# Remainder queries of a head pair: two 64-column products side by side, or one of full width

## The chip, the core and the metric

The kernel runs as one program on one core of a Trainium2 chip. The metric is the device time of one execution in microseconds, and the kernel before was timed three times: 865.73, 865.88 and 868.37 us, median 865.88. A smaller number is better. One further execution was recorded by the hardware profiler; all rows below come from it.

## The reference

Three stages follow each other. q is pooled over pairs of positions, so each of 4 x 8 heads has 576 queries, 1152 keys and 64 features:

```python
q_pool = q.reshape(B, H, S // 2, 2, D).mean(axis=3)
scores = scale * np.matmul(q_pool, k.transpose(0, 1, 3, 2))
attn = np.exp(scores - scores.max(-1, keepdims=True))
attn = attn / (attn.sum(-1, keepdims=True) + 1e-09)
x = np.matmul(attn, v)            # then (B*S/2, H*D) = (2304, 512)
g = x @ w_gate                    # gated layer, 512 -> 1536 -> 512
x = (g / (1 + np.exp(-g)) * (x @ w_val)) @ w_out
# soft mixture: phi (512 x 32), 8 experts of 512 -> 1024 -> 512, combined per token
```

## The kernel before, in words

**Tiling.** Heads go in 16 pairs, called steps: `(b, p)` with b of 4 batches and p of 4 pairs. The 576 queries of a head are 512, handled as four tiles of 128, and a remainder of 64 (`REM`). The keys are nine chunks of 128. A *unit* is one score tile of up to 512 columns: its products (lines 461 and 462: high and low halves of the numbers, fp16), its exponential on ScalarE (467, `P32`), and the difference between the fp32 exponential and its upper half, `PL`, on GpSimd or VectorE (474). A step has nine units for each head's 512 queries and three for the remainder: in these, a unit holds three key chunks, and of each chunk 64 columns for head 0 and 64 columns for head 1, side by side.

**Weights times values.** The exponentials are then the stationary operand (keys on partitions, queries as columns) and the values move. For the 512 queries that is `pv`, three products of 65 or 64 columns for each query tile and chunk (505, 506, 507): upper half times high values, upper half times low values, `PL` times high values. Column 65 of the values is a one, so the row sums come along. For the remainder it is `pv_rem` (497): each product has 64 stationary columns, those of head 0 write partitions 0 to 63 of slot 4 of the accumulator `acc`, those of head 1 partitions 64 to 127, and the two heads' products are issued in turn. A few units skip the split and take fp32 operands in one product.

**Finish and turn.** After head 1's last product `finish` (520 on) divides by the row sums on VectorE (535 to 537), rounds to fp16 on ScalarE (`xh`, through `cast`, line 211) and takes the rest on VectorE (`xl`, 547). Five ticks later `turn` moves tokens from partitions to columns: the 512 queries by a DMA transpose (576), the remainder by four TensorE transposes of 64 x 64 (586: two halves of the number, two heads), one per quadrant of the array, and one ScalarE copy of the result into the tile `xT` of the gated layer.

**Order.** The program order of each engine is made by a scheduler at build time from the priorities of the units, from `later(n, ...)` (n ticks on) and `not_before`. TensorE takes in turn the scores, the weights times values, the row maxima of the step after next (380), and from step 4 on the gated layer of finished tokens (738 to 743, 811, 816). Engines execute in that order. `acc` has one PSUM bank (`PVB` is 1), so the next head's first `pv` waits until `finish` has read it. The transposes and the logits of the gated layer share one bank (`tr`).

The stationary tile of an instruction stands in the rows as 128*128 or 128*64: contraction rows times stationary columns.

Of the kernel before, what the change touches and what calls it, by code (L numbers as in the profile page):

```python
# [10 lines left out]
F16 = mybir.dt.float16  # L11
F32 = mybir.dt.float32
# [5 lines left out]
ALU = mybir.AluOpType  # L18
# [59 lines left out]
def tile_pool_attention_glu_softmoe(  # L78
# [52 lines left out]
    def not_before(ins, lead):  # L131

        if len(marks) > lead >= 0:
            after(ins, marks[-1 - lead])
# [133 lines left out]
    def split_pair(b, p, first=None):  # L268
        if not first and (b, p) not in highs:
            split_high(b, p)  # L270
        kr, qr, vr = raw[b, p]
        i = (b * NP + p) % NKQ
        KL = KLs[i]
        VV = at.tile([P, 2, NCH, 2, D + 1], F16, tag="VV", bufs=2, name=f"VV{b}_{p}")
        KK = at.tile([P, 2, S], F16, tag="KK", bufs=2, name=f"KK{b}_{p}")
        QQ = at.tile([P, 2, SQ], F16, tag="QQ", bufs=2, name=f"QQ{b}_{p}")
        QH = at.tile([D + 1, 2, SQ], F16, tag="QH", bufs=2, name=f"QH{b}_{p}")
        QHs[b, p] = QH
        for hd in range(2):
            st[b, p, hd] = (KK[:, hd, :], KL[:, hd, :], QQ[:, hd, :], QH[:, hd, :], VV[:, hd], vr[:, hd])  # L280
        if first:
            first_split(*first, KK[:, 0, :], KL[:, 0, :], QQ[:, 0, :], QH[:, 0, :])
            maxima(9)

        if first:
            split_high(b, p, first)
        del raw[b, p]
        r, qp, kh, qh, q_cast = highs.pop((b, p))
        ql = at.tile([P, SQ], F16, tag="ql", bufs=1, name=f"ql{b}_{p}")
        q_low = sub("l", b, p).tensor_tensor(out=ql[r], in0=qp, in1=qh[r], op=ALU.subtract).ins.name  # L290
        kl = at.tile([P, S], F16, tag="kl", bufs=1, name=f"kl{b}_{p}")
        k_low = nc.gpsimd.tensor_tensor(out=kl[r], in0=kr[r], in1=kh[r], op=ALU.subtract)
# [183 lines left out]

    def pv_rem(acc, PH, PL, b, p, parts):

        for i in range(0, len(parts), 2):
            c = parts[i][1]  # L480
            todo = []
            for z in range(2):
                dst = acc[z * D:(z + 1) * D, 4, :]
                VV, vr = st[b, p, z][4:]
                q = slice((i + z) * REM, (i + z + 1) * REM)
                if PL is None:
                    todo.append([(dst, PH[:, q], vr[:, c, :])])
                else:
                    todo.append([
                        (dst[:, :D + 1], PH[:, q], VV[:, c, 0, :]),  # L490
                        (dst[:, :D], PH[:, q], VV[:, c, 1, :D]),
                        (dst[:, :D + 1], PL[:, q], VV[:, c, 0, :]),
                    ])
            n = len(todo[0])
            for k in range(n):
                for z in range(2):
                    nc.tensor.matmul(  # L497
                        *todo[z][k], start=False, stop=(c == NCH - 1 and k == n - 1), skip_group_check=True
                    )

    def pv(dst, PH, PL, VV, vr, q, c, first):
        if PL is None:
# [18 lines left out]
    def attn(b, p):  # L521
# [1 line left out]
        acc = {}  # L523

        def finish(hd):
            ns = 4 + hd
            t = acc[hd]
            if hd == 0:
                acc["x"] = at.tile([P, 5, 2, 2, D], F16, tag="xhl", bufs=XB, name=f"xhl{b}_{p}")
            xhl = acc["x"]  # L530
            rs = at.tile([P, 5, 1], F32, tag="rs", bufs=2, name=f"rs{b}_{p}_{hd}")
            x32 = at.tile([P, 5, D], F32, tag="x32", bufs=1, name=f"x32{b}_{p}_{hd}")

            with tc.high_priority(offset=HP_F):
                nc.vector.tensor_scalar(rs[:, :ns, :], t[:, :ns, D:D + 1], EPS * PSC, 1.0 / XSC, ALU.add, ALU.mult)
                nc.vector.reciprocal(out=rs[:, :ns, :], in_=rs[:, :ns, :])
                nc.vector.tensor_tensor(  # L537
                    out=x32[:, :ns, :], in0=t[:, :ns, :D], in1=rs[:, :ns, :].to_broadcast([P, ns, D]), op=ALU.mult
                )
            xh, xl = (xhl[:, :ns, i, hd, :] for i in range(2))  # L540

            def high():
                not_before(cast("x", b, p, xh, x32[:, :ns, :]), 0)

            def low():
                not_before(
                    sub("x", b, p).tensor_tensor(out=xl, in0=x32[:, :ns, :], in1=xh, op=ALU.subtract), 0
                )

            later(2, high)  # L550
            later(3, low)
            if hd:
                later(5, lambda: turn(xhl))

        def pv_unit(parts, PH, PL):
            hd, c, q0, w = parts[-1]
            if q0 < QT:
                VV, vr = st[b, p, hd][4:]
                if c == 0:
                    acc[hd] = ps("pv", [P, 5, D + 1], bufs=PVB, name=f"pv{b}_{p}_{hd}")  # L560
                for q in range(QT // P):
                    pv(acc[hd][:, q, :], PH, PL, VV, vr, slice(q * P, (q + 1) * P), c, c == 0 and q == 0)
            else:
                pv_rem(acc[1], PH, PL, b, p, parts)
            if hd == 0 and c == NCH - 1 and q0 < QT:
                finish(0)
            if hd == 1 and c == NCH - 1 and q0 == QT:
                finish(1)

        def turn(xhl):  # L570

            for g in range(2):
# [9 lines left out]
            tx = ps("tr", [P, 2, REM], F16, bufs=TRB, name=f"tx{b}_{p}")  # L582
            for hl in range(2):
                for z in range(2):
                    r = slice(z * D, (z + 1) * D)
                    not_before(nc.tensor.transpose(tx[r, hl, :], xhl[r, 4, hl, 1, :], id16[r, r]), 0)
            cast("t", b, p, xt_tile(NBLK - 1)[:, p, b // 2, :, b % 2 * REM:b % 2 * REM + REM], tx)
            if p == NP - 1:
                ready.extend(range(len(ready), 2 * (b + 1) if b < B - 1 else NBLK))

# [677 lines left out]
def _layout(q, k, v, moe_w_gate, moe_w_val, moe_w_out, moe2_phi, moe2_w1, moe2_w2):  # L1268
    import numpy as np

    b, h, s, d = q.shape
    vp = v.reshape(b, h // 2, 2, s // 128, 128, d).transpose(0, 1, 4, 2, 3, 5)
# [33 lines left out]
```

## Time and profile before

| | |
|---|---|
| median of three runs | 865.88 us |
| span of the profiled execution (first to last instruction) | 863.9 us |
| mean granted TensorE clock over the span | 0.990 |
| TensorE busy | 816.8 us (95%) in 9952 products |
| VectorE, ScalarE, GpSimd busy | 541.2, 392.5, 414.0 us |

The profiled execution is one execution; its span is 863.9 us, and 2.0 us lie around it if its whole time is the median. In a timeline, the start of the next row less the start of a row is what a product costs its engine, since products overlap; the duration of a product in a row is its way through the array and is longer. A busy share of TensorE therefore also holds time in which the array waits for its own pipeline.

### The profile page before, as it was taken

What the parts mean: (1) busy time and instruction counts of PE and PEld (TensorE: products, weight loads), DVE (VectorE), ACT (ScalarE), POOL (GpSimd) and SP (SyncE); (2) the same over time, 40 slices, a digit from 0 to 9 for tenths busy, and PEclk for the clock granted to TensorE, in tenths of its full rate; (3) what the DMA queues carried; (4) which work ended last, traced back from release to release, by engine and by line L of the source; (5) the groups of instructions that cost most, each with busy time, mean ns of one, the idle gap of its engine ahead of it and who ended that gap; (6) DMA issues with size and microseconds to landing.
All of it is one profiled execution on the core that took longest, in us unless ns stands there. A gap on an engine that the chain in (4) does not pass through costs nothing.

```text
span 863.9 us, 23702 instructions
## 1 busy us (share of the span) xinstructions
PE 816.8 (95%) x9952; PEld 580.0 (67%) x9952; DVE 541.2 (63%) x1060; ACT 392.5 (45%) x739; POOL 414.0 (48%) x380
## 2 busy tenths in 40 slices
PE   5888898999999999999999999999999999998997
PEld 1455566777666767677776777676777777776345
DVE  6878779678888675666657575666723444445223
ACT  3455678677778444343434344344434211212112
POOL 7878667465768545564564556565445100000100
PEclk9999999999999999999999999999999999999998
DMA  6562678959759433424544445324012598457999
GB/s 194 149 153 84 200 214 239 284 127 280 192 173 293 115 61 82 111 76 100 130 115 120 111 107 125 65 26 97 16 28 38 149 292 267 85 165 193 297 290 292
DMA packets 151868, 132.48 MB, mean 153 GB/s; under 512 B 83152, under 2 KB 120720, under 8 KB 151760
## 3 DMA queue, kind: packets, MB, share of 16 engines
q1 hardware_dynamic: 149600, 130.92, 57.8%
q8 instruction: 78, 1.28, 0.6%
q10 hardware_dynamic: 2160, 0.04, 0.1%
q14 instruction: 30, 0.25, 0.1%
HBM read 84.10 MB, written 7.86 MB: 106 GB/s over the span
## 4 chain that ended last, share of the span: by engine, by line
PE 75%; DVE 12%; DMA 7%; ACT 3%; issue 2%; SPq 0%; ACTq 0%; DVEq 0%
PE st L462 7%; PE st L461 7%; PE mx L380 6%; PE g L738 5%; PE g L743 5%; PE g L742 5%; PE v L738 5%; PE v L743 5%; PE v L742 5%; DVE mp L386 3%; PE pv L497 3%; PE pv L505 3%; PE pv L506 3%; PE pv L507 3%; PE hp L1179 2%
## 5 line engine op out<-in xcount | busy, mean ns | idle before, releaser
L474 POOL TENSOR_TENSOR PL<-P 128x512 f16<-128x512 f32 (+1 forms) x311 | 326.0, 1061 | 230.0 <-ACT P L467 227.7
L467 ACT ACTIVATE P<-st 128x512 f32<-128x512 f32 (+1 forms) x336 | 191.4, 582 | 207.0 <-PE st L462 174.1
L386 DVE TENSOR_REDUCE mp<-mx 128x1 f32<-128x512 f32 x270 | 179.9, 684 | 55.9 <-PE mx L380 53.0
L461 PE MATMUL st<-QQ,KK 128*128 128x512 f16 (+1 forms) x576 | 143.7, 291 | 5.1 <-ACT P L467 4.3
L462 PE MATMUL st<-QH,KL 65*128 65x512 f16 (+1 forms) x576 | 144.4, 293 | 2.7 <-DMA QH<-mt 2.7
L505 PE MATMUL pv<-VV,P 128*128 128x65 f16 x1088 | 136.8, 193 | 4.9 <-DVE x L537 4.8
L506 PE MATMUL pv<-VV,P 128*128 128x64 f16 x1088 | 136.7, 195 | 0.0
L507 PE MATMUL pv<-VV,PL 128*128 128x65 f16 x1088 | 134.6, 192 | 0.0
L738 PE MATMUL g<-xT,wgv 128*128 128x256 f16 x432 | 118.6, 275 | 3.3 <-DVE hs L750 3.0
L505 PEld LDWEIGHTS <-P 128*128 128x128 bf16 x1088 | 103.9, 98 | 25.3 <-DVE x L537 6.5
L743 PE MATMUL g<-xT,wgv 128*128 128x256 f16 x432 | 118.5, 274 | 0.5 <-DVE wgv L703 0.5
L742 PE MATMUL g<-xT,wgv 128*128 128x256 f16 x432 | 118.6, 274 | 0.0
L738 PE MATMUL v<-xT,wgv 128*128 128x256 f16 x432 | 117.9, 273 | 0.0
L743 PE MATMUL v<-xT,wgv 128*128 128x256 f16 x432 | 117.8, 273 | 0.0
L742 PE MATMUL v<-xT,wgv 128*128 128x256 f16 x432 | 117.7, 273 | 0.0
L507 PEld LDWEIGHTS <-PL 128*128 128x128 f16 x1088 | 103.7, 99 | 13.5 <-issue 4.4
L506 PEld LDWEIGHTS <-P 128*128 128x128 bf16 x1088 | 103.2, 98 | 10.4 <-issue 2.2
L380 PE MATMUL mx<-kh,QD 128*128 128x512 f16 x270 | 103.8, 402 | 6.6 <-DVE mp L386 3.1
L738 PEld LDWEIGHTS <-wgv 128*128 128x128 f16 x864 | 85.1, 98 | 18.6 <-issue 2.1
L742 PEld LDWEIGHTS <-wgv 128*128 128x128 f16 x864 | 84.8, 98 | 18.4 <-issue 4.1
L743 PEld LDWEIGHTS <-wgv 128*128 128x128 f16 x864 | 84.8, 98 | 16.1 <-issue 0.8
L462 PEld LDWEIGHTS <-KL 65*128 65x128 f16 x576 | 51.7, 99 | 33.0 <-issue 14.9
(184 smaller groups left out, 1192.4 us busy)
## 6 DMA issues: line engine op xcount, KB each, us to landing
w<-in_w SPq DMA_DIRECT2D x16, 1024.0 KB, 7.6
w<-in_w SPq DMA_DIRECT2D x64, 256.0 KB, 5.5
vr<-in_vP SPq DMA_DIRECT2D x16, 585.0 KB, 5.1
KK<-kh SPq DMA_DIRECT2D x62, 144.0 KB, 2.6
qr<-in_qT SPq DMA_DIRECT2D x15, 576.0 KB, 3.9
kr<-in_kT SPq DMA_DIRECT2D x15, 576.0 KB, 4.2
r<-in_w_out SPq DMA_DIRECT2D x12, 512.0 KB, 4.3
r<-in_w_gate SPq DMA_DIRECT2D x24, 256.0 KB, 5.1
```

Source lines behind the costliest of these rows:

```text
L380: nc.tensor.matmul(t, q, kh[:, k0:k0 + kw], start=True, stop=True)
L386: nc.vector.reduce_max(out=mp[:, g, c:c + 1], in_=t, axis=AX.X)
L461: nc.tensor.matmul(t[:, o:o + w], KK[:, k], QQ[:, q0:q0 + w], start=True, stop=False)
L462: nc.tensor.matmul(t[:, o:o + w], KL[:, k], QH[:, q0:q0 + w], start=False, stop=True)
L467: marks.append(nc.scalar.activation(P32[:, :o], t[:, :o], AF.Exp, scale=1.0 / 16.0).ins.name)
L474: eng.tensor_tensor(out=PL[:, :o], in0=P32[:, :o], in1=PH[:, :o], op=ALU.subtract)
L505: nc.tensor.matmul(dst[:, :D + 1], PH[:, q], VV[:, c, 0, :], start=first, stop=False, skip_group_check=True)
L506: nc.tensor.matmul(dst[:, :D], PH[:, q], VV[:, c, 1, :D], start=False, stop=False, skip_group_check=True)
L507: nc.tensor.matmul(dst[:, :D + 1], PL[:, q], VV[:, c, 0, :], start=False, stop=(c == NCH - 1), skip_group_check=True)
L738: mm = nc.tensor.matmul(o, w[:, 0, d, f], xh, start=(d == 0), stop=False)
L742: nc.tensor.matmul(o, w[:, 0, d, f], xl, start=False, stop=False)
L743: nc.tensor.matmul(o, w[:, 1, d, f], xh, start=False, stop=(d == ND - 1))
```

## The change

The values of the two heads of a pair are stored in reversed order (`_layout`), and `st` keeps the tile of both heads. `pv_rem` now takes all 128 columns of a chunk as stationary operand, and both heads' values (2 x 65 or 2 x 64 columns) move, so that `acc` has six slots: slot 4 holds the values of head 1, slot 5 those of head 0, and of each only one half of the partitions is used afterwards. `finish(1)` divides six slots, rounds the sixth on ScalarE and takes its rest on GpSimd, each in an instruction of its own. `turn` makes two transposes of 128 x 128 in place of four of 64 x 64, and two copies of 64 partitions in place of one of 128.

```diff
-            todo = []
-            for z in range(2):
-                dst = acc[z * D:(z + 1) * D, 4, :]
-                VV, vr = st[b, p, z][4:]
-                q = slice((i + z) * REM, (i + z + 1) * REM)
...
-                        (dst[:, :D + 1], PH[:, q], VV[:, c, 0, :]),
-                        (dst[:, :D], PH[:, q], VV[:, c, 1, :D]),
-                        (dst[:, :D + 1], PL[:, q], VV[:, c, 0, :]),
+        VV, vr = st[b, p, 1][4:]
+        dst = acc[:, 4:, :]
...
+            q = slice(i * REM, (i + 2) * REM)
+                    (dst, PH[:, q], VV[:, :, c, 0, :]),
+                    (dst[:, :, :D], PH[:, q], VV[:, :, c, 1, :D]),
+                    (dst, PL[:, q], VV[:, :, c, 0, :]),
...
-            ns = 4 + hd
+            ns = 4 + 2 * hd
...
-            xh, xl = (xhl[:, :ns, i, hd, :] for i in range(2))
+            nm = 4 + hd
+            xh, xl = (xhl[:, :nm, i, hd, :] for i in range(2))
+            rh, rl = (xhl[:, 4, i, 0, :] for i in range(2))
 
             def high():
+                if hd:
+                    not_before(cast("x", b, p, rh, x32[:, nm, :]), 0)
             def low():
+                if hd:
+                    not_before(nc.gpsimd.tensor_tensor(out=rl, in0=x32[:, nm, :], in1=rh, op=ALU.subtract), 0)
...
             for hl in range(2):
-                for z in range(2):
-                    r = slice(z * D, (z + 1) * D)
-                    not_before(nc.tensor.transpose(tx[r, hl, :], xhl[r, 4, hl, 1, :], id16[r, r]), 0)
-            cast("t", b, p, xt_tile(NBLK - 1)[:, p, b // 2, :, b % 2 * REM:b % 2 * REM + REM], tx)
+                not_before(nc.tensor.transpose(
+                    tx[:, hl].rearrange("p z n -> p (z n)"), xhl[:, 4, hl].rearrange("p z d -> p (z d)"), id16
+                ), 0)
+            for z in range(2):
+                r = slice(z * D, (z + 1) * D)
+                cast("t", b, p, xt_tile(NBLK - 1)[r, p, b // 2, :, b % 2 * REM:b % 2 * REM + REM], tx[r, :, z, :])
```

Line numbers shift by four after `pv_rem`: its products stand at 493 (before 497), those of `pv` at 501 to 503 (before 505 to 507).

The order on TensorE at the first remainder unit of step (3, 1), before: `P_1_18` and `PL_1_18` are the unit's exponentials, `st_2_1` a score tile of the next step, and a size of 64x65 is 64 partitions by 65 columns.

```order
L461 LDWEIGHTS KK_2_9943
L461 MATMUL st_2_1_10855<-QQ_2_9944,KK_2_9943 128x512
L497 LDWEIGHTS P_1_18_10671
L497 MATMUL pv_1_1_10496<-VV_1_9076,P_1_18_10671 64x65
L462 LDWEIGHTS KL_101
L462 MATMUL st_2_1_10855<-QH_2_9945,KL_101 128x512
L497 LDWEIGHTS P_1_18_10671
L497 MATMUL pv_1_1_10496<-VV_1_9076,P_1_18_10671 64x65
```

One product of the unit stands alone between two score products, and the others follow in pairs. The same unit of the changed kernel on TensorE (`lp` are logits of the gated layer):

```order
L820 LDWEIGHTS W2S
L820 MATMUL lp_4_10508<-hs_4_10396,W2S 32x256
L493 LDWEIGHTS P_1_18_10351
L493 MATMUL pv_1_1_10176<-VV_1_8808,P_1_18_10351 128x130
L493 LDWEIGHTS P_1_18_10351
L493 MATMUL pv_1_1_10176<-VV_1_8808,P_1_18_10351 128x2x64
L493 LDWEIGHTS PL_1_18_10353
L493 MATMUL pv_1_1_10176<-VV_1_8808,PL_1_18_10353 128x130
```

Each pair became one product of 128 partitions by 130 or 128 columns, and the unit stands together behind the logits.

The order on TensorE at the turn of step (3, 0), before (`tx` is the result, `xhl` the two halves of the quotient):

```order
L506 MATMUL pv_1_0_10137<-VV_1_9076,P_1_1_10013 128x64
L507 LDWEIGHTS PL_1_1_10015
L507 MATMUL pv_1_0_10137<-VV_1_9076,PL_1_1_10015 128x65
L586 LDWEIGHTS xhl_0_9542
L586 MATMUL tx_0_10182<-id_66,xhl_0_9542 64x64
```

The other three transposes of the turn follow there at once. The second transpose of the same turn in the changed kernel, forty rows behind the first:

```order
L503 MATMUL pv_1_0_9818<-VV_1_8808,PL_1_3_9792 128x65
L586 LDWEIGHTS xhl_0_9248
L586 MATMUL tx_0_9863<-id_66,xhl_0_9248 128x128
L461 LDWEIGHTS KK_1_8809
L461 MATMUL st_1_7_9955<-QQ_1_8810,KK_1_8809 128x512
```

The two transposes of a turn were separated, and the second, which reads what GpSimd makes, stands behind the products of chunk 3.

The order on GpSimd at the same turn in the changed kernel (`VV_2` is the low half of the values of the next step):

```order
L474 TENSOR_TENSOR PL_1_4_9808<-P_1_4_9806 128x512
L308 TENSOR_TENSOR VV_2_9648<-vr_2_9049,VV_2_9648 128x18x64
L474 TENSOR_TENSOR PL_1_5_9876<-P_1_5_9874 128x512
L550 TENSOR_TENSOR xhl_0_9248<-x_0_1_9780,xhl_0_9248 128x64
L474 TENSOR_TENSOR PL_1_6_9919<-P_1_6_9917 128x512
```

Line 550 is the new subtraction; the rows around it are those of before.

## Rows read from the trace of the kernel before

**Rows 1.** busy time by stretch; columns: stretch, length, each engine's busy us

```profile
0.00:150.00 150.00, 123.06 (x1498) 78.69 (x1499) 118.05 (x195) 89.64 (x163) 113.24 (x105) 0.97 0.62 176
150.00:300.00 150.00, 144.76 (x1924) 104.27 (x1923) 121.42 (x223) 107.40 (x206) 95.48 (x82) 1.00 0.77 208
300.00:691.00 391.00, 388.50 (x4895) 286.33 (x4893) 234.75 (x463) 161.87 (x304) 202.77 (x178) 1.00 0.38 88
```

**Rows 2.** longest TensorE wait, 300 to 700 us

```profile
PE mx L380 <- DVE mp L395: 0.8, 2, 0.4
```

**Rows 3.** busy time by stretch of line 497 alone

```profile
0.00:150.00 150.00, 4.66 (x160) 3.51 (x160) 0.97 0.62 176
150.00:300.00 150.00, 8.19 (x230) 5.76 (x228) 1.00 0.77 208
300.00:691.00 391.00, 22.31 (x458) 13.86 (x458) 1.00 0.38 88
```

**Rows 4.** groups by line and shape: xcount | busy us, mean ns | idle before

```profile
L497 PE MATMUL pv<-VV,P 128*64 128x65 f16 x270 | 24.5, 202 | 0.0
L497 PE MATMUL pv<-vr,P 128*64 128x65 f32 x36 | 2.1, 232 | 0.0
L586 PE MATMUL tx<-id,xhl 64*64 64x64 f16 x64 | 5.5, 208 | 0.3 <-DVE xhl L547 0.3
L505 PEld LDWEIGHTS <-P 128*128 128x128 bf16 x1088 | 103.9, 98 | 25.3 <-DVE x L537 6.5 <-issue 3.8 <-DVE xhl L547 0.2
```

**Rows 5.** TensorE timeline, one batch of remainder products; columns: start us, us, what

```profile
588.76 0.22 PE L497 MATMUL pv<-VV,P 128*64 128x65 f16 x1
588.91 0.39 PE L462 MATMUL st<-QH,KL 65*128 65x512 f16 x1
589.23 0.25 PE L497 MATMUL pv<-VV,P 128*64 128x65 f16 x3
...
589.39 0.22 PE L497 MATMUL pv<-VV,PL 128*64 128x65 f16 x2
...
589.49 0.22 PE L497 MATMUL pv<-VV,PL 128*64 128x65 f16 x2
589.64 0.65 PE L380 MATMUL mx<-kh,QD 128*128 128x512 f16 x2
```

**Rows 6.** TensorE timeline, full-width products of different kinds in succession

```profile
309.80 0.38 PE L461 MATMUL st<-QQ,KK 128*128 128x512 f16 x1
310.01 0.38 PE L462 MATMUL st<-QH,KL 65*128 65x512 f16 x1
310.23 0.19 PE L505 MATMUL pv<-VV,P 128*128 128x65 f16 x1
310.26 0.19 PE L506 MATMUL pv<-VV,P 128*128 128x64 f16 x1
```

**Rows 7.** TensorE timeline, full-width products of 128 columns (line 837)

```profile
795.31 0.62 PE L837 MATMUL warm<-id 128*128 128x128 f16 x8
...
797.43 1.07 PE L837 MATMUL warm<-id 128*128 128x128 f16 x16
```

**Rows 8.** TensorE timeline, the four small transposes of one turn

```profile
360.69 0.19 PE L507 MATMUL pv<-VV,PL 128*128 128x65 f16 x1
360.82 0.25 PE L586 MATMUL tx<-id,xhl 64*64 64x64 f16 x4
361.00 0.20 PE L505 MATMUL pv<-VV,P 128*128 128x65 f16 x1
```

**Rows 9.** groups by line and shape, other engines, around finish and turn

```profile
L537 DVE TENSOR_TENSOR x<-pv,rs 128x320 f32<-128x320 f32 x16 | 7.8, 486 | 0.3
L211 ACT COPY xT<-tx 128x128 f16<-128x128 f16 x16 | 4.3, 267 | 5.9 <-PE tx L586 5.9
```

**Rows 10.** GpSimd timeline before a turn

```profile
553.59 1.28 POOL L474 TENSOR_TENSOR PL<-P 128x512 f16<-128x512 f32 x1
```

**Rows 11.** TensorE timeline after the same turn

```profile
555.82 0.19 PE L507 MATMUL pv<-VV,PL 128*128 128x65 f16 x1
```

More of the change, by code (lines that the diff above doesn't have):

```diff
@@ L279, in split_pair @@
         for hd in range(2):
-            st[b, p, hd] = (KK[:, hd, :], KL[:, hd, :], QQ[:, hd, :], QH[:, hd, :], VV[:, hd], vr[:, hd])
+            st[b, p, hd] = (KK[:, hd, :], KL[:, hd, :], QQ[:, hd, :], QH[:, hd, :], VV, vr)
         if first:
@@ L477, in pv_rem @@
     def pv_rem(acc, PH, PL, b, p, parts):
+        VV, vr = st[b, p, 1][4:]
+        dst = acc[:, 4:, :]
         for i in range(0, len(parts), 2):
             c = parts[i][1]
-            todo = []
-            for z in range(2):
-                dst = acc[z * D:(z + 1) * D, 4, :]
-                VV, vr = st[b, p, z][4:]
-                q = slice((i + z) * REM, (i + z + 1) * REM)
[L486 to L489, printed above, removed]
-                        (dst[:, :D + 1], PH[:, q], VV[:, c, 0, :]),
-                        (dst[:, :D], PH[:, q], VV[:, c, 1, :D]),
-                        (dst[:, :D + 1], PL[:, q], VV[:, c, 0, :]),
-                    ])
-            n = len(todo[0])
-            for k in range(n):
-                for z in range(2):
-                    nc.tensor.matmul(
-                        *todo[z][k], start=False, stop=(c == NCH - 1 and k == n - 1), skip_group_check=True
-                    )
+            q = slice(i * REM, (i + 2) * REM)
+            if PL is None:
+                todo = [(dst, PH[:, q], vr[:, :, c, :])]
+            else:
+                todo = [
+                    (dst, PH[:, q], VV[:, :, c, 0, :]),
+                    (dst[:, :, :D], PH[:, q], VV[:, :, c, 1, :D]),
+                    (dst, PL[:, q], VV[:, :, c, 0, :]),
+                ]
+            for k, t in enumerate(todo):
+                nc.tensor.matmul(
+                    *t, start=False, stop=(c == NCH - 1 and k == len(todo) - 1), skip_group_check=True
+                )
     def pv(dst, PH, PL, VV, vr, q, c, first):
@@ L530, in finish @@
             xhl = acc["x"]
-            rs = at.tile([P, 5, 1], F32, tag="rs", bufs=2, name=f"rs{b}_{p}_{hd}")
-            x32 = at.tile([P, 5, D], F32, tag="x32", bufs=1, name=f"x32{b}_{p}_{hd}")
+            rs = at.tile([P, 6, 1], F32, tag="rs", bufs=2, name=f"rs{b}_{p}_{hd}")
+            x32 = at.tile([P, 6, D], F32, tag="x32", bufs=1, name=f"x32{b}_{p}_{hd}")
             with tc.high_priority(offset=HP_F):
@@ L539, in finish @@
                 )
-            xh, xl = (xhl[:, :ns, i, hd, :] for i in range(2))
+            nm = 4 + hd
+            xh, xl = (xhl[:, :nm, i, hd, :] for i in range(2))
+            rh, rl = (xhl[:, 4, i, 0, :] for i in range(2))
             def high():
-                not_before(cast("x", b, p, xh, x32[:, :ns, :]), 0)
+                not_before(cast("x", b, p, xh, x32[:, :nm, :]), 0)
+                if hd:
+                    not_before(cast("x", b, p, rh, x32[:, nm, :]), 0)
             def low():
                 not_before(
-                    sub("x", b, p).tensor_tensor(out=xl, in0=x32[:, :ns, :], in1=xh, op=ALU.subtract), 0
+                    sub("x", b, p).tensor_tensor(out=xl, in0=x32[:, :nm, :], in1=xh, op=ALU.subtract), 0
                 )
+                if hd:
+                    not_before(nc.gpsimd.tensor_tensor(out=rl, in0=x32[:, nm, :], in1=rh, op=ALU.subtract), 0)
             later(2, high)
@@ L557, in pv_unit @@
             if q0 < QT:
-                VV, vr = st[b, p, hd][4:]
+                VV, vr = (x[:, 1 - hd] for x in st[b, p, hd][4:])
                 if c == 0:
-                    acc[hd] = ps("pv", [P, 5, D + 1], bufs=PVB, name=f"pv{b}_{p}_{hd}")
+                    acc[hd] = ps("pv", [P, 6, D + 1], bufs=PVB, name=f"pv{b}_{p}_{hd}")
                 for q in range(QT // P):
@@ L581, in turn @@
                 cast("t", b, p, x, tx)
-            tx = ps("tr", [P, 2, REM], F16, bufs=TRB, name=f"tx{b}_{p}")
+            tx = ps("tr", [P, 2, 2, REM], F16, bufs=TRB, name=f"tx{b}_{p}")
             for hl in range(2):
-                for z in range(2):
-                    r = slice(z * D, (z + 1) * D)
-                    not_before(nc.tensor.transpose(tx[r, hl, :], xhl[r, 4, hl, 1, :], id16[r, r]), 0)
-            cast("t", b, p, xt_tile(NBLK - 1)[:, p, b // 2, :, b % 2 * REM:b % 2 * REM + REM], tx)
+                not_before(nc.tensor.transpose(
[4 more added lines that the diff above has]
+                cast("t", b, p, xt_tile(NBLK - 1)[r, p, b // 2, :, b % 2 * REM:b % 2 * REM + REM], tx[r, :, z, :])
             if p == NP - 1:
@@ L1271, in _layout @@
     b, h, s, d = q.shape
-    vp = v.reshape(b, h // 2, 2, s // 128, 128, d).transpose(0, 1, 4, 2, 3, 5)
+    vp = v.reshape(b, h // 2, 2, s // 128, 128, d)[:, :, ::-1].transpose(0, 1, 4, 2, 3, 5)
     return {
```

## The prediction

> **What bounds the kernel now.** I read the busy time by stretch first. TensorE is busy 123 of the first 150 us, 145 of the next 150 and 388.5 of the 391 us from 300 to 691 [rows 1]. The reader is to see that the other engines have room in the long third stretch: VectorE 235, GpSimd 203, ScalarE 162 of 391. The waits come second: between 300 and 700 us the longest thing that TensorE waited for adds up to 0.8 us [rows 2]. So from 300 us on TensorE's own queue sets the pace, from 150 us nearly so, and in the first 150 us others hold it up too. Busy doesn't mean streaming, though, so I went on to the timeline and took the time from one start to the next as a product's price.
>
> Full-width products cost what their columns cost: two of 512 columns stand 0.22 us apart, one of 65 columns 0.03 us before the next, and going from line 462 to line 505 adds nothing [rows 6]. At the remainder it is different. The line 462 product at 588.91 has 512 columns as well, but the next, 64 stationary columns wide, starts 0.32 us later: 0.10 us too late. The last pair starts at 589.49 (its second product some ns on) and the next full-width product at 589.64, 0.15 us for a pair that costs 0.03 us inside the batch: 0.12 too much. The product alone at 588.76 pays both for one product's work [rows 5]. The small transposes do the same: 0.13 us from a 65-column product into them, 0.10 over its price [rows 8]. So each change between the full and a divided array costs about 0.10 us, and TensorE counts it as busy.
>
> **What the change removes.** Counted in the program's order, the width of the array changes 541 times before and 297 times after. Of the 244 that go, 214 lie at the ends of 107 batches of line 497 and 46 at those of 23 batches of transposes; 16 are not won, since the neighbour there is a narrow product too (the logits, as in the order shown: the change into the logits stays). At 0.10 us that is -24.4 us; with 0.12 on leaving it would be -26.8, and I keep the lower price.
>
> The Trainium skill, in TensorEngine Tiling (Array Packing), Tiling Modes, says that changing the mode drains the engine, which names the cause; it gives no price.
>
> **What it adds on TensorE.** Two products side by side become one with twice the moving columns, so the packing is given up. Before, the pairs run together: from 589.39 to 589.49 lies one chunk, three pairs, 33 ns a pair [rows 5]. There are three fp16 groups of 270 products [rows 4], 810 in all, 405 pairs: 13.4 us. After, 405 products of 130 or 128 columns. Sixteen products of 128 columns take 1.07 us and eight 0.62, which is 56 ns each [rows 7]; the row of 512 columns scaled to 130 gives 56, and two 65-column products in a row 60 [rows 6]. I take 57: 23.1 us, bounds 22.5 and 25. That is +9.7. The fp32 remainder has 36 records, 18 pairs [rows 4], whose spacing no row shows alone: between nothing and twice the fp16 difference, 0 to +2 us; +0.5, near the fp16 rows. Four small transposes take 0.18 us with the way out [rows 8], so 0.08 without; 16 turns are 1.3 us, against 32 full transposes at 56 ns, 1.8: +0.5.
>
> Together on TensorE: -24.4 + 9.7 + 0.5 + 0.5 = -13.7 us.
>
> A rule speaks against this. TensorE: Matmul & The Clock Gate, Back-to-back issue gap, in the Trainium skill puts a sustained stream of weight loads and 128-column products at about 81 ns each, not 56. The line 837 rows alternate loads and products and stand at 56 ns [rows 7], so the trace doesn't agree here. By the rule the 405 products would take 32.8 us and the sum on TensorE be -4.0.
>
> **The other engines.** ScalarE gets a second copy per turn, 0.267 us for the full one and no less assumed for half the partitions, and a rounding of 64 columns, between nothing and the same 0.267 of 128 columns [rows 9]; 16 times both is up to 8.5 us, on an engine that is busy 162 of 391 us. GpSimd gets 16 subtractions of 64 columns, each between nothing and the 1.28 us of 512 columns [rows 10]; near 0.2 by share. On VectorE the product with the row sums grows from 320 to 384 columns: at most 0.1 us more on 0.486 [rows 9]. Three places could reach TensorE. The accumulator's one bank is held 0.1 us longer per step; scores and the gated layer stand in TensorE's queue meanwhile and hide it; uncovered it costs 1.6 us. The `tr` bank is held for the second copy, 0.27 us; the logits behind it wait only if they are next, 4.3 us if always. The second transpose now waits for GpSimd. Behind it stand all later products on TensorE, so this one is dangerous. In the trace of before, the GpSimd row that stands ahead of the new subtraction of step (3, 0) ends at 553.59 + 1.28 = 554.87, so its result is there at about 555.1; TensorE comes to the transpose's new place, behind the products of chunk 3, at 555.82 [rows 10, 11]: 0.7 us of slack. I laid the new order over the old times for all 16 turns; this is the tightest, others have about 2 to 5 us. The copies, the bank and this wait together I take at +0.8, between 0 and 6. SP's queue gets nothing new, and no DMA is added.
>
> **What reaches the end.** Line 497's busy time lies with 4.7, 8.2 and 22.3 us in the three stretches [rows 3]: 13, 23 and 63%. In the first, where TensorE idles 27 of 150 us [rows 1], I let half be lost: 0.9 of 1.8. In the second 15%, 0.5 of 3.2. In the third all counts, since nothing else is near its limit; what is late next there is the row maxima on VectorE, which already end that 0.8 us. From 691 us on no changed instruction runs, and the stretch starts when TensorE has finished the gated layer, so it moves up as a whole. -13.7 + 1.4 + 0.8 = -11.5. The profiled execution spans 863.9 us, and 2.0 lie around it up to the median 865.9; so 852.4 in the profile and 854.4 as time.
>
> **Rivals.**
> *The other engines take part of it.* Row maxima, exponentials and GpSimd set the pace up to 300 us, so that only 63% of 13.7 is won: 8.6 us, and less with all small waits: 857.3, up to 863. For it: VectorE is busy 121 of the 150 us in the second stretch. Against: so is TensorE 145.
> *The wide product costs more.* Each needs a load of 128 x 128 weights, which takes 98 ns [rows 4] and goes on beside the product ahead. If it is only half hidden beyond 57 ns, a product costs 78, and 405 lose 8.5 us of the 11.5: 862.9; wholly bare, at 98, 871. Against it: 65-column products with the same loads stand 30 ns apart [rows 6]. For it: no row has 130 columns from two places. The Trainium skill's 81 ns (the section above) would give 864.1.
> *GpSimd makes it slower.* Place: the second transpose of each turn. If one more difference of 1.28 us slips ahead of the new subtraction and the slack is gone, each turn stalls TensorE by 1.28 us: 16 turns, +20.5 and -11.5, 874.9. It decides from a stall of 0.72 us per turn. Against it stands the slack above.
> *The change doesn't remove the stall.* If the 0.10 us belonged not to the width but to what `pv_rem` reads or writes, 10.7 us of wider products would be added for nothing: 876.6. Against it: lines 505 to 507 read the same kind of tile and accumulate in the same bank without it [rows 6], and the transposes, which read something else, show it [rows 8].
>
> **How the numbers follow.** Forecast 0.75, its own range 850.5 to 858. The other engines 0.14, the wide product 0.05, GpSimd 0.04, no removal 0.02. A measurement of this kernel can tell about 0.3%, 2.6 us, from no change, so faster ends at 863.3: the forecast and the first rival, 0.89. The wide product straddles that edge and I count it as no change, 0.05; slower are the last two, 0.06. With both prices at their better end (0.12 on leaving, 22.5 us, nothing lost) it is some 849, with the small waits at their worse end 861; the range is 849.5 to 861.
>
> **What would show it.** Right: TensorE products of the remainder, 414 in the program, 128*128 with 130 columns, some 57 ns apart, with 0.22 us and not 0.32 between a 512-column product and the first of a batch; TensorE's span from 300 us to the last remainder shorter by about 9 us. The step on GpSimd is wrong if a wait of the transposes for the new subtraction stands in TensorE's list of waits with more than 1 us. The forecast is wrong if the remainder products stand 80 ns apart, or if the idle time of TensorE before 300 us grows by more than 3 us.

## The result, and the profile after

The change makes the kernel faster. Over 18 runs of each the median went from 865.81 to 861.53 us (852.71 to 866.75), 4.3 us less; the ratio is **0.9908, 95% interval 0.9885 to 0.9931**, which is 8.0 us, 6.0 to 10.0. All ratios here and below leave out the runs marked as slow: 865.62 and 866.75 us of after, 874.54 of before (beside experiments 9 and 10) and 2658.91 us in experiment 7. The forecast was 854.4, 11.5 us less than before, so the direction held and 3.5 us are missing by the ratio, 7.1 by the median, which lies half a us above the range's upper end, 861.0. The spread is itself a result. The three of the 18 runs whose mean granted clock of TensorE was 0.989 took 852.7, 852.9 and 853.9 us, 12 to 13 below before; those at 0.974 to 0.979 took 861 to 867. The profiled one is of the second kind: clock 0.975, span 863.3 us, time 865.11, against 0.990 and a span of 863.9 in the profiled execution of before. Its trace has to be read with that in mind: at almost the same length it shows the gain and what takes it back side by side.

First the same stretches as in [rows 1], in after (columns as there).

```profile
0.00:150.00 150.00, 123.62 (x1359) 79.75 (x1360) 110.70 (x186) 85.79 (x158) 109.01 (x104) 0.93 0.61 171
150.00:300.00 150.00, 142.23 (x1802) 105.04 (x1799) 123.60 (x227) 114.03 (x224) 101.97 (x89) 0.99 0.72 206
300.00:691.00 391.00, 387.10 (x4729) 295.42 (x4727) 240.37 (x474) 165.95 (x324) 208.06 (x189) 0.99 0.41 95
```

The granted clock (third figure from the end) is 0.93 in the first stretch where it was 0.97. As the work moves against fixed stretches, they don't show what a piece of it costs. So I cut both traces at two points of the program: VectorE's product of the accumulator with the row sums in the 8th and in the 16th (last) step. TensorE alone, before; columns: stretch, length, busy us, clock, DMA share, GB/s.

```profile
0.00:306.40 306.40, 274.22 (x3482) 0.98 0.69 190
306.40:676.90 370.50, 369.38 (x4698) 1.00 0.37 83
676.90:863.90 187.00, 173.23 (x1776) 0.98 0.85 233
```

The same between the same points, after.

```profile
0.00:310.40 310.40, 276.25 (x3250) 0.96 0.67 188
310.40:669.90 359.50, 358.22 (x4479) 1.00 0.38 85
669.90:863.30 193.40, 177.74 (x1773) 0.95 0.81 225
```

In the middle, at full clock, after is 11.0 us shorter, and all of that is busy time (369.4 to 358.2). Up to the 8th step it is 4.0 longer: 2.0 of busy time at a lower clock, 2.0 of idle time. From the last step on it is 6.4 longer, 4.5 of it busy time at clock 0.95 instead of 0.98, though only the last of the 16 turns was changed there. -11.0 + 4.0 + 6.4 = -0.6, the difference of the spans. (Up to the first point 324 products of the gated layer are done where before had 333; at 0.11 us each that is 1 us of work moved into the middle.)

The products themselves came out as forecast. TensorE's timeline in after, a batch between products of the gated layer (columns as in [rows 5]):

```profile
667.84 0.27 PE L746 MATMUL g<-xT,wgv 128*128 128x256 f16 x1
667.94 0.22 PE L493 MATMUL pv<-VV,PL 128*128 128x130 f16 x1
668.00 0.28 PE L493 MATMUL pv<-VV,P 128*128 128x130 f16 x2
668.12 0.22 PE L493 MATMUL pv<-VV,PL 128*128 128x130 f16 x1
...
668.35 0.28 PE L493 MATMUL pv<-VV,P 128*128 128x130 f16 x2
668.47 0.27 PE L747 MATMUL g<-xT,wgv 128*128 128x256 f16 x1
```

The 256-column product ahead takes 0.10 us, no more than between two of its kind, and leaving the batch costs nothing over the last product's own price. Nine products from 667.94 to 668.47 are 59 ns each here, and over the trace the median from one to the next is 58. In [rows 5] the way in cost 0.10 and the way out 0.12. It is so throughout the middle: from a 512-column score product to the first product of a batch the median is 0.22 us in after (25 places) and 0.32 in before (47). The small transposes are gone as a stall too; a turn's first transpose in after, which answers to [rows 8]:

```profile
595.38 0.19 PE L503 MATMUL pv<-VV,PL 128*128 128x65 f16 x1
595.41 0.22 PE L586 MATMUL tx<-id,xhl 128*128 128x128 f16 x1
595.47 0.38 PE L380 MATMUL mx<-kh,QD 128*128 128x512 f16 x1
```

0.03 us before it and 0.06 for it, nothing else. Counted in the order of the trace, the array's width changes 583 times before and 340 times after: 243 fewer (the forecast had 244, from the program's order).

The groups that answer to [rows 4, 9], after (columns as there): the wide products, the turn's copies and transposes, GpSimd's new subtraction and the product on VectorE.

```profile
L493 PE MATMUL pv<-VV,P 128*128 128x130 f16 x135 | 26.5, 219 | 0.0
L533 DVE TENSOR_TENSOR x<-pv,rs 128x384 f32<-128x384 f32 x16 | 8.8, 552 | 0.3
L211 ACT COPY xT<-tx 64x128 f16<-64x128 f16 x32 | 8.2, 257 | 5.6 <-PE tx L586 5.4
L550 POOL TENSOR_TENSOR xhl<-x,xhl 128x64 f16<-128x64 f32 x16 | 7.4, 460 | 4.9 <-ACT xhl L211 4.9
L586 PE MATMUL tx<-id,xhl 128*128 128x128 f16 x32 | 6.7, 223 | 0.8 <-ACT xhl L211 0.4 <-POOL xhl L550 0.3
```

And what TensorE waited for between 300 and 672 us, after, which answers to [rows 2] (columns: total us, times, longest):

```profile
PE g L742 <- DVE hs L754: 0.8, 2, 0.4
PE tx L586 <- ACT xhl L211: 0.4, 1, 0.4
PE tx L586 <- POOL xhl L550: 0.3, 1, 0.3
```

GpSimd's subtraction takes 0.46 us, more than twice my share of the 512 columns, and still TensorE waits for it once in this window, 0.3 us. The two waits of the transposes here belong to the last turn, at 671 and 672 us; between the 8th and the 16th step no transpose waits. The dangerous place of the forecast costs next to nothing.

### The profile page after: what moved, and what is told of

Its sections match the earlier page's. It is cut to its first block, busy times and chain, and to the rows that moved or that the text cites. A ratio compares the mean times of both kernels' runs of the same rounds, so it can differ in the third digit from the quotient of the medians.

```text
span 863.3 us, 22875 instructions
## 1 busy us (share of the span) xinstructions
PE 812.2 (94%) x9497; PEld 590.4 (68%) x9497; DVE 540.4 (63%) x1060; ACT 399.4 (46%) x771; POOL 421.6 (49%) x396
## 4 chain that ended last, share of the span: by engine, by line
PE 71%; DVE 11%; DMA 9%; ACT 3%; issue 2%; POOL 1%; SPq 1%; ACTq 0%; DVEq 0%; POOLq 0%
PE st L462 6%; PE st L461 6%; PE g L742 5%; PE g L747 5%; PE g L746 5%; PE v L742 5%; PE v L747 5%; PE v L746 5%; PE mx L380 5%; DVE mp L386 3%; DMA r<-in_w_val 3%; DMA r<-in_w_out 3%; PE pv L501 3%; PE pv L502 3%; PE pv L503 2%
## 5 line engine op out<-in xcount | busy, mean ns | idle before, releaser
L467 ACT ACTIVATE P<-st 128x512 f32<-128x512 f32 (+1 forms) x336 | 191.4, 581 | 196.0 <-PE st L462 158.9
L461 PE MATMUL st<-QQ,KK 128*128 128x512 f16 (+1 forms) x576 | 145.8, 292 | 8.3 <-ACT P L467 7.9
L462 PE MATMUL st<-QH,KL 65*128 65x512 f16 (+1 forms) x576 | 147.3, 295 | 1.6 <-DMA QH<-mt 1.5
L501 PE MATMUL pv<-VV,P 128*128 128x65 f16 x1088 | 139.7, 195 | 4.5 <-DVE x L533 4.4
L502 PE MATMUL pv<-VV,P 128*128 128x64 f16 x1088 | 139.4, 197 | 0.0
L503 PE MATMUL pv<-VV,PL 128*128 128x65 f16 x1088 | 137.7, 194 | 0.1
L501 PEld LDWEIGHTS <-P 128*128 128x128 bf16 x1088 | 105.7, 100 | 23.6 <-DVE x L533 6.3
L502 PEld LDWEIGHTS <-P 128*128 128x128 bf16 x1088 | 104.7, 99 | 12.4 <-issue 3.0
L742 PEld LDWEIGHTS <-wgv 128*128 128x128 f16 x864 | 85.4, 99 | 18.3 <-issue 1.8
L747 PEld LDWEIGHTS <-wgv 128*128 128x128 f16 x864 | 85.2, 99 | 17.4 <-DVE wgv L707 1.3
```

Source lines behind the costliest of these rows:

```text
L461: nc.tensor.matmul(t[:, o:o + w], KK[:, k], QQ[:, q0:q0 + w], start=True, stop=False)
L462: nc.tensor.matmul(t[:, o:o + w], KL[:, k], QH[:, q0:q0 + w], start=False, stop=True)
L467: marks.append(nc.scalar.activation(P32[:, :o], t[:, :o], AF.Exp, scale=1.0 / 16.0).ins.name)
L501: nc.tensor.matmul(dst[:, :D + 1], PH[:, q], VV[:, c, 0, :], start=first, stop=False, skip_group_check=True)
L502: nc.tensor.matmul(dst[:, :D], PH[:, q], VV[:, c, 1, :D], start=False, stop=False, skip_group_check=True)
L503: nc.tensor.matmul(dst[:, :D + 1], PL[:, q], VV[:, c, 0, :], start=False, stop=(c == NCH - 1), skip_group_check=True)
```

## Where the missing part is: what the trace of after suggests

Two things differ outside the changed lines: TensorE's clock, and the waits ahead of its slower stretches. First the clock. TensorE's stretches at the lower of its two levels add up to 18.1 us of the span in before and 42.5 in after. Windows around two of after's stretches, TensorE alone:

```profile
100.00:108.00 8.00, 8.00 (x86) 0.57 0.64 180
672.00:684.00 12.00, 10.15 (x61) 0.72 0.82 216
```

The same windows in before, at full clock:

```profile
100.00:108.00 8.00, 6.19 (x78) 1.00 0.52 138
672.00:684.00 12.00, 10.61 (x139) 1.00 0.33 74
```

In such a stretch a product costs twice its price: from 675.46 us on in after, the 256-column products stand 0.21 to 0.22 us apart, where they stand 0.11 apart at full clock. A fully busy engine thus loses half of the stretch, and 24.4 us more of it are up to 12 us, an estimate: enough for all that is missing in the profiled run.

The times on record say the same. At a mean clock of 0.989, after took 852.7 to 853.9 us and before 861.4 to 867.5 (13 runs, timed beside the experiments; median 865.7): 12 us apart. At 0.983, after took 857.5 to 860.0; at 0.982 to 0.984 before took 867.2 to 871.7: some 10 apart. At like clock the change is worth about what was forecast. But after's runs have a mean clock of 0.981 and before's beside the experiments of 0.987. By these two figures some 11 us more are at the lower level, which is up to 5 us of time, an estimate.

Now the waits. Each of the two stretches at half clock follows a wait; that the wait brings it about is not shown by that. The first begins on ScalarE, whose timeline in after, 92 to 99 us, is (in brackets: idle before it, and what released it):

```profile
96.92 0.65 ACT L652 ACTIVATE r<-r 128x512 f32<-128x512 f32 x1 [2.95 <-DMA r<-in_w_out]
97.48 0.60 ACT L655 ACTIVATE lo<-r 128x512 uint32<-128x512 uint8 x1
98.02 0.58 ACT L467 ACTIVATE P<-st 128x512 f32<-128x512 f32 x1
```

and on TensorE, next to it:

```profile
95.87 0.22 PE L380 MATMUL mx_r<-kh,QD 128*128 128x128 f16 x1
98.65 0.38 PE L461 MATMUL st<-QQ,KK 128*128 128x512 f16 x1 [2.56 <-ACT P L467]
```

ScalarE takes its instructions in order. It stands for 2.95 us at a weight tile of the gated layer whose DMA has not landed; the exponential behind it starts at 98.02, and the next scores stand until the bank is read: 2.56 us without a product. Two us later the half-clock stretch begins. Here are ScalarE's waits for such loads, 60 to 310 us, before:

```profile
ACT r L648 <- DMA r<-in_w_val: 11.2, 13, 2.0
ACT r L648 <- DMA r<-in_w_out: 6.2, 6, 2.4
```

and after:

```profile
ACT r L652 <- DMA r<-in_w_out: 14.6, 8, 2.9
ACT r L652 <- DMA r<-in_w_val: 9.8, 11, 2.0
ACT r L652 <- DMA r<-in_w_gate: 1.6, 1, 1.6
```

17.4 us became 26.0. The second place is the last turn, where no other work is left to lie over its chain. TensorE, after:

```profile
671.18 0.23 PE L586 MATMUL tx<-id,xhl 128*128 128x128 f16 x1 [0.40 <-ACT xhl L211]
671.73 0.23 PE L586 MATMUL tx<-id,xhl 128*128 128x128 f16 x1 [0.32 <-POOL xhl L550]
672.58 0.30 PE L815 MATMUL lp<-hs,W2S 128*64 128x256 bf16 x2 [0.62 <-ACT xT L211]
...
673.61 0.71 PE L850 MATMUL L<-La,SELW 128*32 128x256 f32 x2 [0.52 <-DVE La L826]
675.08 0.37 PE L742 MATMUL g<-xT,wgv 128*128 128x256 f16 x1 [0.76 <-DMA xT<-xhl]
```

The same place in before:

```profile
678.46 0.22 PE L586 MATMUL tx<-id,xhl 64*64 64x64 f16 x2 [0.31 <-DVE xhl L547]
679.04 0.30 PE L811 MATMUL lp<-hs,W2S 128*64 128x256 bf16 x2 [0.36 <-ACT xT L211]
...
680.07 0.62 PE L846 MATMUL L<-La,SELW 128*32 128x256 f32 x2 [0.52 <-DVE La L822]
680.89 0.27 PE L738 MATMUL g<-xT,wgv 128*128 128x256 f16 x1 [0.20 <-DMA xT<-xhl]
```

The waits are 2.6 us in after and 1.4 in before. In after the clock is at half from about 674 us on, behind the first 1.9 of them (the window from 672 us above); before kept the full clock.

So **theory A**: the whole saving on TensorE is there, and part of it is given back where ScalarE stands behind late loads and where TensorE's clock is then lower. **Theory B**: the new turn (its wait for GpSimd, two copies, two more small instructions) costs what is missing.

## The experiments

All compute the whole output. Each ratio is to the kernel before, timed beside it on the same chip, with its 95% interval.

**1 and 2: one part alone.** The first keeps the turn of before and takes only the wide products (with one more product on VectorE to bring the second head's half into its place); the second keeps the pairs of 64 columns and takes only the new turn.

```diff
 # experiment 1, against after (excerpts)
+                nm = 4 + hd
...
+                if hd:
+                    nc.vector.tensor_tensor(
+                        out=x32[:D, 4, :], in0=t[:D, 5, :D], in1=rs[:D, 5, :].to_broadcast([D, D]), op=ALU.mult
+                    )
...
+                for z in range(2):
+                    r = slice(z * D, (z + 1) * D)
+                    not_before(nc.tensor.transpose(tx[r, hl, :], xhl[r, 4, hl, 1, :], id16[r, r]), 0)
 # experiment 2, against after (excerpts)
...
+            for z in range(2):
+                dst = acc[z * D:(z + 1) * D, 4, :]
...
+                        (dst[:, :D + 1], PH[:, q], VV[:, c, 0, :]),
+                        (dst[:, :D], PH[:, q], VV[:, c, 1, :D]),
+                        (dst[:, :D + 1], PL[:, q], VV[:, c, 0, :]),
...
```

> The wide products alone: finish writes head 0's rows of the sixth slot over the fifth, and the turn is that of before (four 64x64 transposes, one copy, nothing new on GpSimd). Theory A (all of the saving on TensorE's queue is there, and a lower granted clock takes part back): of 244 changes of width about 200 go, -20 us, and the wider products add 10, so about -10 us before the clock, and 857 to 862 us as timed with 20 to 40 us at half clock. Theory B (the new turn over ScalarE and GpSimd costs waits at each step, and that is what is missing): with the old turn back it is faster than the full change, 853 us or less, with a mean clock near 0.989 as before.

> The new turn alone: the remainder products are the 64-wide pairs of before; the fp16 halves are written twice so that two 128x128 transposes and two copies can follow. Theory A: 46 changes of width less, -4.6 us, +0.5 for the longer transposes, so 861 to 865 us. Theory B: the waits of the new turn show without the gain, 866 to 872 us, with TensorE waiting more than 5 us in total for the transposes' inputs or behind the copies.

The wide products alone: 863.29 us, **0.9965 [0.9939, 0.9991]**, just above theory A's range; the turn alone: 876.90, over by 10 us, **1.0121 [1.0090, 1.0152]**, above the ranges of both theories. By that, B looks right, though the kernel with the old turn isn't the faster one that B asked for. But the trace doesn't put those 10 us at the turns. Between the 8th and 16th step the turn alone takes 368.9 us where before takes 370.5; up to the 8th it is 314.0 instead of 306.4, with 40.7 us of idle TensorE instead of 32.2; from the last step on it takes 192.7 at clock 0.94 instead of 187.0 at 0.98. What TensorE waited for up to the 8th step, experiment 2:

```profile
PE st L461 <- ACT P L467: 7.7, 13, 1.3
...
PE v L745 <- ACT r L681: 3.6, 1, 3.6
...
PE tx L589 <- ACT xhl L211: 0.8, 1, 0.8
```

The exponentials (4.3 us in before) and one weight tile of the gated layer, 3.6 us, stand there; the transposes of the turn wait 0.8. The verdict has to come from kernels in which the loads are taken out of the way.

**3: the last turn covered.** A few pieces of the gated layer are kept back and put around the last transposes (two in each of two ticks), so that TensorE has work there.

```diff
-MOE_PACE = [(4, 0.0), (8, 1.0), (16, 6.1)]
+MOE_PACE = [(4, 0.0), (8, 1.0), (15.5, 5.78), (16, 5.8)]
...
+                if (b, p) == steps[-1]:
+                    after(tr, moe["mm"])
...
+    for k in range(LOAD_LAG):
+        if k in (3, 4):
+            for _ in range(2):
+                next(moe_work)
+        tick()
```

> The full change, with the last turn put behind some products of the gated layer, of which a few are kept back for it (pace 5.8 blocks in place of 6.1 at the end). Theory A: TensorE's waits of 2.6 us at the last turn go, and with them the 6.8 us at half clock behind it (3.4 us of time): 3 to 6 us faster than the full change, 852 to 858 us. Theory B: the last turn is one of 16, so 0 to 1 us faster.

859.05 us, **0.9922 [0.9894, 0.9950]**, between the two theories and not to be told from after. The half-clock stretch at the last turn is gone, but three waits of 1.2 to 1.4 us stand at 671, 705 and 720 us instead. In the profiled execution TensorE takes 191.4 us from the last step on, at clock 0.99 and with 29 products more (some 3 us of work moved in), against 193.4 in after. What the last turn's stretch costs by itself is not settled by this.

**4 and 5: ScalarE's conversion later.** The conversion of a weight tile is issued six ticks behind the load it needs instead of at once, so that the exponentials don't stand behind it; all that follows from the tile moves by six ticks too. Once on after, and once, as the control, on before.

```diff
+        return r, out, sc
...
+    CONV_LAG = 6
...
+    def conv_out(r, out, sc):
...
-        w = conv(conv_place(False), None, srcs, 2.0).rearrange("p (a n) -> p a n", a=2)
+        got = conv(conv_place(False), None, srcs, 2.0)
...
+        later(CONV_LAG, lambda: kept.append(conv_out(*got).rearrange("p (a n) -> p a n", a=2)))
...
-        later(3, halves)
+        later(3 + CONV_LAG, halves)
...
-        later(4, turned)
+        later(4 + CONV_LAG, turned)
```

> The full change, with ScalarE's part of the conversion of the gated layer's weights put six ticks behind the loads, so that exponentials no longer queue behind a load that has not landed. Theory A: the wait of 2.6 us of TensorE for an exponential in step 2 goes, and with it the half clock between 100 and 120 us: 3 to 6 us faster than the full change. If the clock fell there for another reason (the accumulator's hand-over), no more than 2 us. Theory B: no change.

> The kernel before with ScalarE's conversion six ticks behind the loads (the edit of the fourth experiment alone). ScalarE waited 17 us for those loads in the kernel before, 26 us in the changed one, 7 us with the edit. Theory A (the change saves some 12 us of TensorE, and part of it is eaten where ScalarE stands behind a load): the kernel before gains less from the edit than the changed one, 856 to 860 us, so that with the edit on both sides the change is worth 10 to 13 us. Theory B (the gain of the fourth experiment is an order that came out well by chance): 848 to 853 us here, the change worth less than 5 us.

On after: 847.26 us (846.14 to 847.78), **0.9783 [0.9754, 0.9812]**. On before: 863.81, **0.9973 [0.9949, 0.9997]**. One edit is worth 2.3 us without the change and about 11 with it, more than the 3 to 6 expected; the control lies above the ranges of both theories. ScalarE's waits for loads, 60 to 310 us, in the first of the two:

```profile
ACT r L658 <- DMA r<-in_w_out: 6.7, 3, 3.8
```

6.7 where after had 26.0. The wait of 2.56 us and the half clock behind it are gone: TensorE is busy through 96 to 100 us (1.2 of these 4 us in after), its longest wait for an exponential is 1.4 us, and the clock is full from 62.5 to 130 us. TensorE's first stretch, up to the same point of the 8th step, and the middle, there:

```profile
0.00:286.40 286.40, 256.54 (x3177) 0.98 0.71 199
286.40:654.20 367.80, 366.52 (x4553) 1.00 0.38 87
```

The clock up to the 8th step is back at 0.98. (Of its 24 us, some 7 are work that moved: fewer products of the gated layer, 259 instead of 324, are done by then, and stand in the middle. The sum up to the 16th step, 654.2 against 669.9, holds equal work.) With the loads out of the way the change is worth 0.9783 / 0.9973 = 0.981: about -16 us, some 3 us either way if the two intervals are combined as independent. The clock is only part of what the edit gives to the changed kernel: at a mean clock of 0.989 experiment 4 took 846.1 us, and after 852.7 to 853.9.

**6 and 7: the parts alone again, with the conversion later** (the edits of 1 and 4, and of 2 and 4).

> The wide products alone (old turn), with the same edit of the conversion. Theory A: 8 to 10 us faster than the kernel before with the edit, so 848 to 852 us. Theory B: within 3 us of it.

> The new turn alone (64-wide pairs), with the same edit of the conversion. Theory A: the 10 us that the new turn alone lost came from waits before 310 us, not from the turn; with the edit it is 1 to 4 us faster than the kernel before with the edit, 853 to 858 us. Theory B: the new turn itself costs, and it is again 6 us or more slower than that kernel.

Wide products: 853.38 us, **0.9849 [0.9823, 0.9874]**. Turn: 862.34, **0.9957 [0.9930, 0.9984]**. Against the control, 0.9973, the wide products are worth -10.7 us and the turn -1.4, no difference within its bounds. As differences these are near what was expected; the times themselves lie above theory A's ranges, as the control's does. The turn that cost 10 us in experiment 2 costs nothing here, with the same instructions: **B falls**, as far as the turn's own instructions go. The width changes in these traces go 595 (control), 378 (wide), 547 (turn), 336 (both). At 0.10 us, with +9.7, +0.5 and +0.5 for what is added, that makes -11.5 for the wide products, -4.3 for the turn and -15.2 for both; measured are -10.7, -1.4 and -16, each to some 3 us. That is the forecast's sum on TensorE, without its losses.

What the conversion's edit gives goes roughly with one wait of TensorE. In the profiled executions its waits for exponentials (40 to 310 us) fall from 7.9 to 2.9 us with the whole change, from 10.8 to 4.6 with the wide products alone and from 6.7 to 3.9 with the turn alone; these three kernels gain 11, 10 and 14 us. In before they don't fall (4.3 and 5.0), though ScalarE's waits for loads do (17.4 to 5.0), and it gains 2.3. Why before's order bore its late loads better is open.

**8: experiments 3 and 4 together.**

> The full change with both edits, the conversion behind the loads and the last turn behind products of the gated layer. Theory A: the two act in different stretches and add, 843 to 846 us. Theory B: within 1 us of the fourth experiment, 846 to 848 us.

846.44 us (lowest 843.01), **0.9767 [0.9739, 0.9795]**: the lowest median of all, and below both kernels, though the cover of the last turn isn't shown to add to experiment 4.

**9 and 10: the loads earlier, the conversion later still.** If late loads are the cause, starting them earlier should do as well; and ten ticks should do as well as six.

```diff
 # experiment 9, against after
-PREP_LEAD = 3
+PREP_LEAD = 9
 # experiment 10, against experiment 4
-    CONV_LAG = 6
+    CONV_LAG = 10
```

> The full change with the loads of the gated layer's weights let go nine units ahead of the newest exponential in place of three; ScalarE's part stays where it was. Theory A (ScalarE stands 26 us behind loads that haven't landed, and the half clock follows from it): the wait falls to under 12 us and the time to 848 to 855 us, in another way than in the fourth experiment. Theory B (the fourth experiment's order came out well by chance): within 3 us of the full change. If the three buffers of these loads hold them back anyway, the wait stays at 20 us or more and nothing moves, which tells nothing.

> The full change with ScalarE's conversion ten ticks behind the loads in place of six. Theory A: the wait for loads was 7 us with six ticks and falls to 4 or less; at most 3 us faster than the fourth experiment, 844 to 848 us. Theory B: another order, another time, anywhere from 845 to 862 us.

Theory A's times missed in both. Earlier loads: 867.81 us, **1.0029 [1.0000, 1.0057]**, slower than after and outside both theories. The wait moved to other loads, and fell only from 26.0 to 18.3 us; ScalarE, 60 to 310 us:

```profile
ACT r L652 <- DMA r<-in_w_val: 18.1, 11, 4.4
ACT r L652 <- DMA r<-in_w_out: 0.2, 1, 0.2
```

and TensorE's wait for exponentials, 40 to 310 us, went from 7.9 us in after to

```profile
PE st L461 <- ACT P L467: 12.5, 18, 1.8
```

with the mean clock at 0.973. With experiment 4 it was 2.9. So the sum of ScalarE's waits for loads (18.3 here, 26.0 in after) doesn't set the time; here the time goes with TensorE's waits for exponentials and with the clock. Those waits don't order all runs either: experiment 2 had 6.7 us of them and took 876.90. Ten ticks: 852.1 us, **0.9861 [0.9808, 0.9915]**. The waits for loads are as good as gone (3.2 us), the clock isn't better than in experiment 4 (0.979 against 0.983 in the profiled ones), and it is some 5 us slower, inside theory B's range. Its six runs spread from 849.55 us at 0.989 to 861.42 at 0.974. Where the conversions fall among the exponentials matters beyond the loads; that part I have not taken apart.

**The tail, over all runs.** In no kernel but 3 and 8 was the order behind the last turn meant to change, yet the stretch from the last step on (the last turn, old or new, stands at its start) is between 187.0 and 193.4 us long in the others. TensorE there in experiment 6 and in the control, 5:

```profile
663.20:850.70 187.50, 173.01 (x1774) 0.98 0.84 232
```

```profile
675.10:866.80 191.70, 177.52 (x1776) 0.95 0.83 227
```

It goes with the clock, not with the change: 187.0 and 187.5 us at 0.98 (before, experiment 6), 189.9 to 191.1 at 0.96 and 0.97 (10, 9, 4), 191.7 to 193.4 at 0.94 and 0.95 (5, 7, 1, 2, after). The control has nothing of the change and the long tail; experiment 6 has the wide products and the short one. Each is one execution.

## Why the prediction was right, and which step of it failed

**The price of a width change, right.** 243 changes fewer, no 0.10 us left at the wide batches, 11.0 us less in the middle stretch at full clock (forecast there 8.6 in its "third stretch", which begins 6 to 10 us earlier), and -10.7 us for the wide products alone in experiment 6. TensorEngine Tiling (Array Packing), Tiling Modes, in the Trainium skill, says that a mode change drains the engine; the 0.10 us at each change fits that, and the page has no price.

**The wide product, right.** 58 ns against 57. The rival that it costs more falls, and so does the Trainium skill's 81 ns (TensorE: Matmul & The Clock Gate, Back-to-back issue gap): 405 loads and products, alternating, don't show it here, and the measured 58 decides.

**The other engines, right as far as the turn goes.** No wait of the transposes in the middle and one for GpSimd of 0.3 us in the last turn; idle TensorE in the middle 1.1 us before and 1.3 after. GpSimd's own 0.2 us was 0.46, VectorE's "at most 0.1 more" 0.07, a copy 0.257 for 0.267. None of the prediction's signs of being wrong came: the products stand 58 ns apart, no wait for GpSimd is near 1 us, and TensorE's idle time before 300 us grew from 32.2 to 34.2 us, by less than 3.

**"In the first ... I let half be lost", failed.** It allowed 1.4 us to be lost before 300 us and expected some 3.6 to be won. In the profiled execution the 8th step comes 4.0 us later instead. The step took the idle time of before as it stands. It did not ask what the faster order does to an engine that serves two masters: ScalarE's queue holds the exponentials and the weight conversions in one order, and in after more exponentials stood behind loads that had not landed. The first rival named this stretch and the exponentials among its actors, but not the loads ahead of them, and it took it only as a loss of the gain, not as a cost.

**"It moves up as a whole", failed.** The tail moved up by 7.0 us and grew by 6.4 in the profiled execution. Behind the last turn no instruction of it was changed, but its clock was 0.95 instead of 0.98. I had read that column in before and left it out of the sum: a stretch in which TensorE is the bound is priced in columns and clock, and the second is not a constant.

The forecast's number is what the kernel does when its clock is as in before (the three runs at 0.989, none of which has a trace), and the mechanism on TensorE was the right one. In the profiled execution, which is among the longest of after, the two terms cost some 14 us against the forecast (4.0 instead of -3.6, 6.4 instead of 0), and the middle gave 2.4 more than the 8.6 that were its share. How the 3.5 to 7 us missing over all runs divide is not shown, since one execution has a trace. That the time still came near the range is in part luck: the forecast has no term for the clock, and with after's clock the same program took anything from 852.7 to 866.8 us. Open remain why the clock in the tail falls in some executions and not in others, what share of the missing part is idle time and what share clock, and what experiment 10 loses against 4.

## What to carry to other kernels

Count the changes of the array's width in TensorE's order, and price each at what the timeline shows on the way in and out; a packed pair that stands alone between full-width products can cost more than one full-width product with twice the columns. Cut two traces at points of the program, not of time, and read the granted clock of each piece beside its busy time before putting a gain or a loss down to the lines that were changed. If a change removes work from the bounding engine and half of it doesn't arrive, try the next-worst wait together with it, with a control that has the wait's edit alone: 2.3 us on one kernel were 11 on the other.

## What the runs showed that I had not expected

The same program took 852.7 us at a mean clock of 0.989 and 865.1 at 0.975. By these two clocks some 24 us more are at the lower level, so up to 12 us of time (an estimate): as much as the two times differ. And a part that costs 10 us in one setting (the new turn, experiment 2) costs nothing in another (experiment 7), with the same instructions: its price was that of the setting. Loads that were issued earlier (experiment 9) didn't help: ScalarE's waits for them fell by 8 us in sum, but it stood 18.1 us at the next kind of load, up to 4.4 at a time, and TensorE's waits for exponentials grew.
